# A new issue order for the first 25 slots of a fused top-k attention and feed-forward kernel

## The chip, the cores and the metric

The kernel runs on one core of one Trainium2 chip. Its five engines work side by side, each with an instruction queue of its own: TensorE (PE) multiplies matrices, VectorE (DVE), ScalarE (ACT) and GpSimd (POOL) work on tiles element by element, and SyncE (SP) issues the transfers. The metric is the device time of one execution in microseconds. PSUM is the memory that TensorE writes its products to, SBUF the memory that the other operands lie in.

## The reference

Two blocks follow each other. The first is attention that keeps, for each query, only the 32 largest of its 576 scores. The second is a feed-forward layer with a quick GELU. All is float32.

```python
B, H, S, D = q.shape                      # 8, 8, 576, 64
scores = scale * np.matmul(q, k.transpose(0, 1, 3, 2))
kth = np.partition(scores, -32, axis=-1)[..., -32:-31]
scores = np.where(scores >= kth, scores, -1000000000.0)
scores = scores - np.max(scores, axis=-1, keepdims=True)
attn = np.exp(scores)
attn = attn / (np.sum(attn, axis=-1, keepdims=True) + 1e-09)
attn_out = np.matmul(attn, v)
x = attn_out.transpose(0, 2, 1, 3).reshape(B * S, H * D)   # 4608 x 512
h = x @ w_in                              # 512 x 2048
g = h * (1.0 / (1.0 + np.exp(-1.702 * h)))
out = g @ w_out                           # 2048 x 512
```

## The kernel before

**Slots.** The attention is cut into 144 slots, each of 128 query rows for two heads. For slot n the work passes through all engines, in these steps (the names are those of the code and of this text):

- scores(n) (L468): matmuls on TensorE into two PSUM banks, named c = 0 and c = 1; a bank holds one half of the keys. In the code the four calls for bank 0, each recorded as one step, come before the four for bank 1; the profile counts two matmuls for each call, 16 in all.
- copy_scores(n) (L482): two copies on ScalarE, one for each bank, to the SBUF tile `sc`.
- pair_up(n) (L489): two instructions on VectorE, which take the maximum and the minimum of each pair of keys, one from bank 0 in PSUM and one from the copy of bank 1. The result is the tile `ranked`. Bank 0 can be written again once pair_up(n) and the copy of bank 0 have both read it.
- topk(n) (L509): 14 instructions on VectorE, four rounds of MAX8 (the eight largest) with a MATCH_REPLACE8 (take them out) behind all rounds but the last, for each of the two heads. The first two rounds work on 288 elements, the later ones on 576.
- bounds(n) (L534) on GpSimd works out the cut and the row maximum, mask(n) (L549) and exps(n) (L557) on ScalarE mask and exponentiate, two instructions each, with the sums.
- invert(n) (L568): one small instruction on GpSimd and a reciprocal on VectorE. Up to slot 7 divide(n) (L575) makes two scaled diagonals of it on GpSimd; from slot 8 on normalize(n) (L582) multiplies the probabilities by it on GpSimd.
- Up to slot 7 turn(n) (L590) transposes the probabilities by matmuls on TensorE. From slot 8 on split(n) (L618) copies them apart into 16-bit halves (ScalarE), a transfer writes them to DRAM (`rows<-sc`), and turn_by_dma(n) (L626) brings them back transposed (`pt<-rows`).
- values(n) (L652) or values_at(n) (L685) multiplies them with v on TensorE, and a copy on ScalarE brings the result to `xT`.

Four slots make a block of 128 rows of x. For each block follow hidden (L789; TensorE, h = x @ w_in, into `ph`, or `unit` from slot 25 on), tanh (L814; ScalarE), gate and combine (L826, L843; GpSimd), project (L896; TensorE) and the store of the block. project makes seven products of quarter matrices in place of eight; the matrices that this takes from w_out are made once, by `part` (L877) on GpSimd, the "matrix sums" of the text below, as `raws<-wout,raws`.

**Stages.** opening (L1109) loads and turns the first q and k. slot (L1174) writes the steps of slots 0 to 10, filling_slot (L1339), called by filling (L1375), those of slots 11 to 20 with find (L1303) for the top-k and values_held (L1318) for two slots' values at a time, steady_pair (L1412) those of 21 to 24. From slot 25 on joined_pair (L1599) issues the work directly, in the order in which it is written. stay_warm (L299) issues matmuls whose result nobody reads.

**The order of the first 25 slots.** What opening, slot, filling and steady_pair call on an engine isn't issued at once. Engine and Engines (L123, L138) record each call as a step, 2593 in all. issue_in_order (L1678) then issues them in the order of the table ORDER (L36): a list of step numbers, in which "a+k" is the run of k steps from a. The numbers are those of the order in which the code calls them. Each engine executes its own steps in the order in which the table has them, and a step waits for whatever it depends on that another engine makes. In the trace all recorded steps carry line L133, those issued directly L132.

The lines that decide the order:

```python
        for part in ORDER.split():
            first, _, count = part.partition("+")
            order += range(int(first), int(first) + int(count or 1))
    assert sorted(order) == list(range(len(steps)))
    for i in order:
        steps[i]()
```

BY_DMA is 8 and SETTLED is 10: slot 8 is the first whose probabilities are turned by a transfer, slot 10 the last that slot (L1174) writes.

Of the kernel before, what the change touches and what calls it, by code (L numbers as in the profile page):

```python
# [145 lines left out]
def kernel(  # L146
# [1228 lines left out]
    def filling():  # L1375
# [20 lines left out]

        gate()
        bring_all()
        filling_slot(11, [copy_qk], [], [lambda: values(BY_DMA + 1, put_off), unit], [])
        finish_all()  # L1400
        summing.extend(all_weight_sums())
        filling_slot(12, [bring_all, th], [sums(1)], [put, put, ends_in_turn], [])
# [335 lines left out]
```

## Time and profile before

| | |
|---|---|
| median of 3 runs | 1343.35 us (1343.03 to 1345.45) |
| the profiled execution's own time | 1344.24 us |
| its span in the trace | 1342.4 us |
| mean granted TensorE clock | 0.997 |
| busy: TensorE, VectorE, ScalarE, GpSimd | 1324.3, 1267.8, 1157.6, 979.1 us |
| transfers over the span | 249.27 MB |

The time of an execution holds 1.84 us beside the span of the profile. A row of the timeline has the start in us from the beginning of the span, the time from the start of the row's first instruction to the end of its last one (a row may join some instructions of one kind, "x2"), the engine, the line, the operation, the tiles out<-in with their sizes, and in square brackets how long the engine had stood idle before and what ended that. A row of the windows has the stretch from:to in us, its length, the busy us and the count of instructions of TensorE's matmuls, TensorE's weight loads, VectorE, ScalarE and GpSimd, the granted clock, the busy share of the transfer engines and their GB/s. A row of the grouped instructions has the count, the busy time and the mean ns of one, and the idle time before. A row of the waits names the waiting engine and tile, the engine and tile that ended the wait, and then the time in us, the number of waits and the mean of one. SPq is the queue in which SyncE issues transfers.

### The profile page before, as it was taken

How to read it: one execution, taken by the hardware profiler on the slowest of the kernel's cores; microseconds unless marked ns; L12 is line 12 of the kernel's file. 1: busy time of each engine (PE TensorE's matmuls, PEld its weight loads, DVE VectorE, ACT ScalarE, POOL GpSimd, SP SyncE). 2: the span in 40 equal slices, each digit the busy share in tenths (PEclk: the TensorE clock that was granted, in tenths of full speed). 3: DMA queues.
4: the chain of work that ended last, by engine and by line, in shares of the span. 5: the costliest groups of instructions: out<-in, count | busy, mean ns of one | idle time of the engine just before them, and what ended most of it. 6: DMA issues, size and time to landing. Idle time of an engine off the chain costs nothing.

```text
span 1342.4 us, 54134 instructions
## 1 busy us (share of the span) xinstructions
PE 1324.3 (99%) x22528; PEld 1202.4 (90%) x22528; DVE 1267.8 (94%) x3371; ACT 1157.6 (86%) x1871; POOL 979.1 (73%) x1788
## 2 busy tenths in 40 slices
PE   7999999999999999999999999999999999999998
PEld 5777579899999999999999999999999999999998
DVE  7999999999999999999999999999999999999902
ACT  6999998999999988999999989899989988888831
POOL 3889887777777777777777777777777777777761
PEclk8999999999999999999999999999999999999999
DMA  8444868798989797988999788998899878755640
GB/s 249 157 143 150 197 169 206 195 208 201 219 215 202 170 206 183 230 198 200 204 230 204 186 169 196 230 190 212 176 234 214 189 170 172 186 146 141 148 115 18
DMA packets 532358, 249.27 MB, mean 186 GB/s; under 512 B 463760, under 2 KB 510352, under 8 KB 532112
## 3 DMA queue, kind: packets, MB, share of 16 engines
q1 hardware_dynamic: 531520, 245.38, 78.9%
q8 instruction: 176, 2.88, 0.9%
q14 instruction: 70, 0.57, 0.1%
q10 hardware_dynamic: 592, 0.43, 0.1%
HBM read 46.01 MB, written 104.60 MB: 112 GB/s over the span
## 4 chain that ended last, share of the span: by engine, by line
PE 90%; DVE 4%; ACT 3%; DMA 1%; POOL 1%; issue 1%; DVEq 0%; POOLq 0%; ACTq 0%
PE unit L132 32%; PE po L132 29%; PE mixed L132 12%; PE s_ps L132 7%; PE po L133 4%; DVE ranked L133 2%; PE ph L133 2%; DVE top L133 2%; PE s_ps L133 2%; PE o L133 1%; ACT sc L133 1%; PE tp L133 1%; DMA xT<-rows 1%; ACT raws L133 1%; ACT pr L133 1%
## 5 line engine op out<-in xcount | busy, mean ns | idle before, releaser
L132 DVE MAX8 top<-ranked 128x8 f32<-128x288 f32 (+1 forms) x952 | 517.7, 595 | 0.0
L132 PE MATMUL unit<-xT,win 128*64 128x128 f32 x7936 | 454.2, 273 | 0.0
L132 PEld LDWEIGHTS unit<-xT,win 128*64 128x64 f32 x7936 | 437.4, 137 | 0.0
L132 DVE MATCH_REPLACE8 ranked<-top,ranked 128x288 f32<-128x288 f32 x714 | 383.4, 542 | 0.0
L132 PE MATMUL po<-wout,th 128*64 128x128 f32 x4032 | 329.8, 274 | 0.0
L132 POOL TENSOR_TENSOR th<-th,th 128x128 f32<-128x128 f32 x374 | 273.9, 732 | 29.9
L132 PE MATMUL po<-raws,th 128*64 128x128 f32 x3064 | 252.7, 273 | 0.0
L132 PEld LDWEIGHTS po<-wout,th 128*64 128x64 f32 x4032 | 238.1, 137 | 9.9 <-issue 5.5
L132 POOL TENSOR_SCALAR pr<-pr,rden 128x576 f32<-128x576 f32 x240 | 176.5, 746 | 75.1 <-DVE rden L132 74.4
L132 ACT COPY sc<-pr 128x2304 uint16<-128x2304 uint16 x96 | 205.5, 2141 | 0.9 <-POOL pr L132 0.8
L132 PEld LDWEIGHTS po<-raws,th 128*64 128x64 f32 x3064 | 184.4, 137 | 0.0
L132 ACT ACTIVATE th<-unit 128x512 f32<-128x512 f32 x124 | 74.9, 604 | 94.3 <-PE unit L132 94.3
L132 ACT ACTIVATE pr<-sc,low 128x576 f32<-128x576 f32 x192 | 148.2, 787 | 0.0
L132 ACT ACTIVATE sc<-sc,cut 128x576 f32<-128x576 f32 x192 | 140.8, 797 | 0.0
L132 POOL TENSOR_SCALAR some<-den 128x2 f32<-128x2 f32 x120 | 26.4, 220 | 155.8 <-ACT pr L132 155.4
L132 PE MATMUL s_ps<-qk_t 64*64 64x512 f32 x936 | 139.1, 596 | 0.0
L132 DVE TENSOR_TENSOR ranked<-s_ps,sc 128x576 f32<-128x576 f32 x188 | 132.6, 747 | 0.0
L132 ACT COPY sc<-s_ps 128x1024 f32<-128x1024 f32 x93 | 95.6, 1028 | 33.7 <-PE s_ps L132 32.7
L132 POOL TENSOR_TENSOR th<-th 128x128 f32<-128x128 f32 x250 | 114.7, 459 | 0.4
L133 DVE MAX8 top<-ranked 128x8 f32<-128x576 f32 (+1 forms) x200 | 111.6, 593 | 0.1
L132 POOL TENSOR_TENSOR raws<-raws 128x128 f32<-128x128 f32 (+1 forms) x160 | 89.7, 569 | 8.1 <-ACT raws L132 3.0
L132 POOL TENSOR_SCALAR th<-th 128x512 f32<-128x512 f32 x124 | 76.6, 618 | 13.2 <-ACT th L132 13.1
(145 smaller groups left out, 2178.9 us busy)
## 6 DMA issues: line engine op xcount, KB each, us to landing
rows<-sc SPq DMA_DIRECT2D x112, 576.0 KB, 3.8
rows<-spare SPq DMA_DIRECT2D x24, 576.0 KB, 3.7
qk_rows<-pr SPq DMA_DIRECT2D x23, 576.0 KB, 5.4
out_dram<-raws SPq DMA_DIRECT2D x66, 128.0 KB, 3.3
raws<-in_moe_w_in_dram SPq DMA_DIRECT2D x16, 512.0 KB, 4.9
raws<-in_moe_w_out_dram SPq DMA_DIRECT2D x16, 512.0 KB, 3.9
qk_l<-in_q_dram SPq DMA_DIRECT2D x28, 256.0 KB, 4.9
qk_l<-in_k_dram SPq DMA_DIRECT2D x28, 256.0 KB, 4.6
```

What stands on the lines that cost most here:

```text
L132: return do(*args, **kwargs)
L133: self.engines.collected.append(lambda: do(*args, **kwargs))
```

## The change

The table ORDER gets other contents from about its 120th step on; its first steps and the recorded steps themselves stay, and so does all that is issued directly from slot 25 on. It is a permutation of the same 2593 steps. Counted for each engine, 1171 of TensorE's 1376 steps stand at another place of its queue, 401 of VectorE's 462, 279 of ScalarE's 353, 232 of GpSimd's 273, and none of SyncE's 129. In one line of filling `BY_DMA + 1` becomes `SETTLED - 1`; both are 9. The table has 81 changed lines, of which six from its beginning and two from its end are shown for each side.

```diff
@@ -36,87 +36,87 @@
 ORDER = """
 8 11 0+8 9 12 10 13+5 22 18 23+2 33 25 19 26+5 20 31 34 32 21 38+4 97 35+3 98 42+8 99 50 54+2 100 56+4 53 51
...
-89 133+4 106 96 123 111 124 138+4 107 112 108 125 137 142 126 143 109 144 110 145 127 146+9 128 155 129 163
-208+4 130 156 162 157 167 131 166 158 191 132 175 168 192 171 212 177 159 218 176 172+3 170 182 160 178 213+4
-161 194 169 179+3 183 219 221+2 184 164 185 193 190 195 217 237 224 264 238 226 186 197 189 223 198+3 239 220
-196 266 225 290 227+3 205 230+4 202 307 234+3 204 267 244 269 259+3 265 245 201 308 187 274 291 165 206 293 188
-240 207 251+4 273 289 262 361 275 246+4 255 360 287 241 294 268 250 276 311 280 242 322 366 323+2 256 243 203
-312+3 303 315+4 288 281 309 270+3 340 371 370 358 325 283 326 282 292 327 362 257 263 328 333 329 284 373 258
...
-2562 2561 2563 2572+8 2486 2591+2 2487 2516+2 2590 2564+8 2587 2488 2588 2518+2 2528+2 2489 2589 2530+2 2520+2
-2532+2 2583+2
+89 133+4 106 96 123 111 138+4 107 124 112 108 125 137 126 142 109 143 110 144 127 145+6 128 151+4 162 155 129
+156 130 213+4 163 157 166 131 208+4 194 217 191 132 168 192 158 167 172+3 171 159 175 170 212 176 264 161 218
+177 179+3 195 220 169 221+2 182 230+4 219 223 178 198+3 266 265 160 193 184 237 234+3 245 238 183 185 226 165
+239 190 315+4 186 197 164 227+3 273 224 188 196 290 187 307 189 205 244 246+4 202 225 204 251+4 267 201 259+3
+275 341 269 206 293 291 263 289 411+4 280 241 270+3 361 262 287 274 277+3 282 255 207 362 240 360 370 250 294
+358 268 296 322+2 243 324+4 276 311+4 242 397 297+3 301 309 203 283 304 359 328 288 319+3 284 450 366 281 256
...
+2504 2528+2 2591 2508+2 2485 2510+2 2592 2582 2542 2556+4 2486 2562+2 2552+4 2487 2572+8 2587 2488 2564+8 2588
+2590 2530+2 2589 2489 2512+8 2532+2 2520+2 2583+2
@@ -1396,7 +1396,7 @@
 
         gate()
         bring_all()
-        filling_slot(11, [copy_qk], [], [lambda: values(BY_DMA + 1, put_off), unit], [])
+        filling_slot(11, [copy_qk], [], [lambda: values(SETTLED - 1, put_off), unit], [])
         finish_all()
         summing.extend(all_weight_sums())
         filling_slot(12, [bring_all, th], [sums(1)], [put, put, ends_in_turn], [])
```

146 rows, old and new, of the table ORDER are left out of this document.

## The prediction

> **What bounds the kernel now.** I read the page's shares first, then the windows by stage, then the waits of single engines, and last the timeline around each wait that is left.
>
> ```profile
> span 1342.4 us, 54134 instructions
> PE 1324.3 (99%) x22528; PEld 1202.4 (90%) x22528; DVE 1267.8 (94%) x3371; ACT 1157.6 (86%) x1871; POOL 979.1 (73%) x1788
> PE 90%; DVE 4%; ACT 3%; DMA 1%; POOL 1%; issue 1%; DVEq 0%; POOLq 0%; ACTq 0%
> ```
>
> Two engines are almost full over the whole run, and the chain that ends last is TensorE's. A share over the whole run says little about the first 25 slots, so the next view cuts the span where the work changes.
>
> ```profile
> 112.00:157.00 45.00, 43.87 (x340) 28.39 (x342) 44.97 (x121) 43.83 (x76) 40.07 (x53) 1.00 0.63 173
> 157.00:197.00 40.00, 37.46 (x542) 30.31 (x538) 40.00 (x108) 37.23 (x65) 34.46 (x55) 1.00 0.81 187
> 197.00:247.00 50.00, 49.86 (x948) 45.25 (x952) 48.69 (x131) 44.28 (x70) 38.15 (x71) 1.00 0.77 186
> 247.00:1250.00 1003.00, 1002.80 (x18262) 935.48 (x18256) 1000.65 (x2656) 897.22 (x1409) 736.88 (x1414) 1.00 0.87 196
> ...
> DVE rden L132 <- POOL some L132: 1.7, 6, 0.3
> ```
>
> The columns are PE, PEld, VectorE, ScalarE, GpSimd. From 112 to 197 VectorE is the one that is full (44.97 of 45, 40.00 of 40). From 197 on TensorE is full as well, and from 247 (slot 25, untouched by the change) both are: 1002.80 and 1000.65 of 1003. VectorE waits there six times, 1.7 us in all. So what the new table wins or loses shows at the end one for one, as the time at which TensorE and VectorE together enter slot 25. A win on one of the two alone is worth nothing.
>
> What is there to win? These are VectorE's waits behind the opening:
>
> ```profile
> 32.08 0.76 DVE L133 TENSOR_TENSOR ranked<-s_ps,sc 128x576 f32<-128x576 f32 x1 [0.54 <-ACT sc L133]
> 82.34 0.76 DVE L133 TENSOR_TENSOR ranked<-s_ps,sc 128x576 f32<-128x576 f32 x1 [0.96 <-ACT sc L133]
> 102.01 0.76 DVE L133 TENSOR_TENSOR ranked<-s_ps,sc 128x576 f32<-128x576 f32 x1 [0.31 <-ACT sc L133]
> 221.03 0.76 DVE L133 TENSOR_TENSOR ranked<-s_ps,sc 128x576 f32<-128x576 f32 x1 [1.15 <-ACT sc L133]
> ...
> DVE rden L133 <- POOL some L133: 0.5, 2, 0.4
> ```
>
> That is 0.54 + 0.96 + 0.31 + 1.15 + 0.5 = **3.5 us**, the most that VectorE can gain: its instructions are the same 462 in both tables, so their sum can't change. 0.2% of the time, about what a measurement can tell from no change, is 2.7 us. Four of the waits are pair_up(n), for n = 3, 8, 10 and 23, waiting for the copied scores. TensorE's own wait, just before it becomes full, is this:
>
> ```profile
> 188.77 1.13 PE s_ps L133 x16
> ...
> 190.52 6.48 DMA pt<-rows
> ...
> 197.83 0.22 PE ph L133 x4
> ...
> 197.14 0.57 PE L133 MATMUL o<-pt,v_l 128*64 128x64 f32 x12 [1.41 <-DMA pt<-rows]
> ```
>
> values_at(16) stands still for **1.41 us** until the transposed probabilities of slot 16 have landed. From there to the end TensorE hardly pauses, so its arrival at slot 25 is this landing plus a fixed amount of work.
>
> **The change part by part.** (a) *The literal* `BY_DMA + 1` becomes `SETTLED - 1`: 8 + 1 and 10 - 1 are both 9, so no instruction changes. Cost nothing. (b) *SP's queue*: the 129 recorded DMA issues stand in the same order in both programs, so no transfer moves past another. (c) *Scores.* In the old table the four matmuls of bank 0 always come before those of bank 1. In the new one bank 1 begins first in 19 of the 24 slots from 2 to 25, and its copy to SBUF often stands early: copy_scores(5) of bank 1 is ScalarE's 55th recorded instruction instead of its 72nd, that of slot 3 its 36th instead of its 41st. Bank 0, which pair_up reads directly, is then all that is still to be made when pair_up of the slot before has freed it. What that took where VectorE waited is in the ends of the pair_ups before the four waits:
>
> ```profile
> 25.57 0.75 DVE L133 TENSOR_TENSOR ranked<-s_ps,sc 128x576 f32<-128x576 f32 x1
> ...
> 75.33 1.41 DVE L133 TENSOR_TENSOR ranked<-s_ps,sc 128x576 f32<-128x576 f32 x2
> ...
> 95.70 0.75 DVE L133 TENSOR_TENSOR ranked<-s_ps,sc 128x576 f32<-128x576 f32 x1
> ...
> 212.93 0.74 DVE L133 TENSOR_TENSOR ranked<-s_ps,sc 128x576 f32<-128x576 f32 x1
> ```
>
> From the end of pair_up(n-1) to the start of pair_up(n): 32.08 - 26.32 = 5.76, 82.34 - 76.74 = 5.60, 102.01 - 96.45 = 5.56, 221.03 - 213.67 = 7.36 us. Against that stands the *room*, VectorE's own work between the two. In the new program it is counted with the durations of
>
> ```profile
> L133 DVE MAX8 top<-ranked 128x8 f32<-128x576 f32 x93 | 67.3, 741 | 0.0
> L133 DVE MATCH_REPLACE8 ranked<-top,ranked 128x288 f32<-128x288 f32 x92 | 40.1, 438 | 0.0
> L133 DVE MAX8 top<-ranked 128x8 f32<-128x288 f32 x91 | 38.8, 443 | 0.1
> L133 DVE MATCH_REPLACE8 ranked<-top,ranked 128x576 f32<-128x576 f32 x46 | 33.9, 738 | 0.0
> ```
>
> each less 0.08 us by which neighbours overlap, a replace with 0.06 us for its load: 0.66, 0.42, 0.36 and 0.72 us. At slot 3 a wide maximum and three narrow replaces are added (0.66 + 3 x 0.42): room up 1.9, the wait of 0.54 goes. At slot 23 three wide maxima, one wide replace and three narrow replaces raise it by 4.0 (3 x 0.66 + 0.72 + 3 x 0.42): the 1.15 goes. At slots 8 and 10 the room falls a little (4.9 to 4.6, 5.4 to 4.6). There it is the early bank 1 that must save 1.0 us; 16 score matmuls take 1.13, so doing half of them and a copy ahead saves about 1.1 to 1.2, an estimate from that row. The 0.96 and 0.31 should go, with little to spare. (d) *Slot 5* gets worse. There bank 0's copy now stands behind the first mask of slot 3:
>
> ```profile
> 50.10 0.24 POOL L133 TENSOR_SCALAR cut<-top 128x4 f32<-128x4 f32 x1
> ...
> 51.07 1.45 ACT L133 ACTIVATE sc<-sc,cut 128x576 f32<-128x576 f32 x2
> ...
> 51.45 0.74 DVE L133 TENSOR_TENSOR ranked<-s_ps,sc 128x576 f32<-128x576 f32 x1
> ```
>
> Half of the masks (0.72) and a copy from 51.07 on end at 52.4, while pair_up(5), with 0.74 us more ahead of it and 0.54 less waiting, would start at 51.65. Bounds: nothing, if ScalarE runs earlier, or 0.7 lost. I take 0.6, since the mask can't start before the cut at 50.34. So VectorE stands 0.54 + 0.96 + 0.31 + 0.4 (the first reciprocal) - 0.6 = 1.6 us earlier at slot 16. (e) *TensorE's wait at 197.* The new order puts all of scores(21) (16 matmuls, 1.13 us) before values_at(16) and two steps of hidden (4 matmuls, 0.22) behind it: 0.91 us of the 1.41 is filled with work. The other 0.5 goes if the landing comes 0.5 us earlier. Its chain:
>
> ```profile
> 175.85 2.52 POOL L133 TENSOR_TENSOR raws<-wout,raws 128x512 f32<-128x512 f32 x2
> ...
> 180.25 0.87 POOL L133 TENSOR_TENSOR th<-th 128x128 f32<-128x128 f32 x2
> ...
> 182.20 1.47 POOL L133 TENSOR_SCALAR pr<-pr,rden 128x576 f32<-128x576 f32 x2 [0.78 <-DVE rden L133]
> ...
> 183.70 2.12 ACT L133 COPY sc<-pr 128x2304 uint16<-128x2304 uint16 x1
> ...
> 185.85 0.35 SPq L133 DMA_DIRECT2D rows<-sc  x1
> ...
> 190.52 2.89 SPq L133 DMA_TRANSPOSE pt<-rows  x1
> ```
>
> GpSimd's normalize(16) gets two more matrix sums ahead and three combining steps fewer (2 x 1.26 - 3 x 0.43 = 1.2 us later), but it had waited 0.78 for the reciprocal. That reciprocal gets two more narrow maxima ahead (0.7), and ScalarE's split(16) one copy fewer. With 1.6 gained on VectorE the reciprocal is 0.9 earlier, GpSimd is late by 1.2 - 0.78 = 0.4 if nothing ahead of it moves, and earlier by up to 0.9 if it follows VectorE. Bounds for the landing: 0.4 later to 1.2 earlier. I take 0.5 earlier, about the middle. So the whole wait of 1.41 goes, and TensorE is then held by its own work. More could come only from its smaller pauses between 150 and 175. (f) *197 to 247* must let VectorE follow. Its 1.15 at slot 23 is there for that.
>
> **Sum:** -0.9 (work into the wait) - 0.5 (earlier landing) = **-1.4 us**. The profiled execution took 1344.24 (span 1342.4), so 1342.8 in its terms; the median of the runs is 0.89 lower, so I predict 1343.35 - 1.4 = **1342.0**.
>
> [...] TensorE's order in slots 1 to 4, warm-up matmuls included, is shuffled most.
>
> ```profile
> 24.00:28.00 4.00, 1.54 (x4) 0.70 (x5) 4.00 (x10) 3.14 (x9) 3.68 (x5) 0.72 0.99 339
> 28.00:32.00 4.00, 4.00 (x23) 2.44 (x23) 3.54 (x9) 3.26 (x7) 3.54 (x7) 0.50 1.05 390
> 32.00:36.00 4.00, 3.90 (x29) 3.27 (x27) 3.92 (x13) 4.00 (x8) 3.26 (x4) 0.93 0.47 184
> 44.81 1.40 DVE L133 TENSOR_TENSOR ranked<-s_ps,sc 128x576 f32<-128x576 f32 x2
> ```
>
> The granted clock falls to 0.72, then 0.50, then is back at 0.93: TensorE is idle there and works at half rate until about 32. The new order has scores(3), half of scores(4) and then nothing until turn(0), so the slow stretch may last to 36. turn(0), 16 matmuls in about 1.8 us there, would take 1.8 longer. Scores(4) has room for that before pair_up(4) at 44.81, but the copies of turn(0) stand in ScalarE's queue ahead of exps(1), and so of the second reciprocal. [...]
>
> **The rivals.** *A, everything fits:* all 3.5 us of VectorE's waits go and TensorE's small pauses shrink too. For: bank 1 ahead is what the four waits lacked. Against: TensorE must gain as much, and only 1.41 of its wait is one piece. Time 1343.35 - 3.2 = 1340.1. *B, no gain:* the slow clock costs VectorE 1.8 less the 0.5 of wait that goes at slot 3, 1.3, or the landing comes no earlier while slot 5 waits. Time 1343.4. *C, slower: rooms too small.* In the new order the room falls from 10.1 to 4.9 at slot 9, 7.5 to 3.4 at 11, 6.3 to 3.6 at 19 and 8.3 to 4.8 at 22. If bank 0 still needed the 5.6 us of slots 8 and 10, because TensorE or ScalarE reaches it late in its own queue, slots 11 and 19 alone would lose 2.2 + 2.0. It decides from the point where bank 0's scores don't start within 2 us of pair_up's end. Time 1343.35 - 1.4 + 4.2 = 1346.2. For: both engines are 93% busy or more between 157 and 197. Against: at 11 and 19 pair_up no longer waits for bank 0's copy, which stands behind it.
>
> **How the numbers follow.** Forecast 0.45 (1340.8 to 1343.0), A 0.18, B 0.19, C 0.18. The range takes in A with all 3.5 us (1339.85) and C's single time: 1339.9 to 1346.2. Faster by over 0.2% (under 1340.66) is A: 0.18. Slower by over 0.2% (over 1346.04) is most of C: 0.15, since C may also cost a little less than its 4.2. The rest, 0.67, is within 0.2%.
>
> **What would show it.** Right: no wait of values_at(16) for the transposed rows, and TensorE full about 1.4 us earlier; no waits at pair_up 3, 8, 10 and 23; a wait of half a microsecond at 5; the first `unit` matmul of slot 25 about 1.4 earlier; the same windows from there. Wrong: new waits of VectorE on the copied scores at 9, 11, 19 or 22 (C), or a granted clock below 0.9 between 32 and 36 with a later second reciprocal (B).

## The result, and the profile after

The changed kernel takes **1346.89 us** (median of 10 executions, 1345.04 to 1351.7) against 1343.40 (10 executions, 1342.73 to 1345.45). The ratio is 1.0029, 95% interval 1.0018 to 1.0039: it is slower, by 0.29% or some 3.9 us (the two medians lie 3.5 apart). Its executions also lie further apart, over 6.7 us in place of 2.7. The profiled execution took 1347.04 us, its span is 1345.2.

First the windows of the changed kernel, with the columns of before:

```profile
112.00:157.00 45.00, 42.57 (x305) 27.56 (x306) 44.62 (x123) 42.65 (x71) 40.61 (x51) 1.00 0.61 173
157.00:197.00 40.00, 39.04 (x556) 31.46 (x556) 38.79 (x104) 37.26 (x67) 34.76 (x54) 1.00 0.82 185
197.00:247.00 50.00, 49.37 (x922) 44.19 (x920) 48.51 (x129) 45.69 (x73) 38.20 (x75) 1.00 0.76 196
247.00:1250.00 1003.00, 1002.52 (x18268) 935.79 (x18266) 1000.49 (x2658) 897.12 (x1410) 734.77 (x1411) 1.00 0.86 196
```

From 247 to 1250 TensorE and VectorE are busy for as long as before, to 0.3 us; TensorE has one new wait there, 0.48 for a landing at 1015. VectorE, full before from 112 to 197, now has gaps (44.62 of 45, 38.79 of 40). So most of this execution's loss must be in the time at which the two engines enter slot 25. These rows are the first pair_up of the execution, pair_up(26) (the first that is issued directly) and the first `unit` matmul; before, then after:

```profile
9.86 1.42 DVE L133 TENSOR_TENSOR ranked<-s_ps,sc 128x576 f32<-128x576 f32 x2 [2.78 <-ACT sc L133]
...
246.24 1.41 DVE L132 TENSOR_TENSOR ranked<-s_ps,sc 128x576 f32<-128x576 f32 x2
...
252.05 3.66 PE L132 MATMUL unit<-xT,win 128*64 128x128 f32 x64
```

```profile
10.62 1.42 DVE L133 TENSOR_TENSOR ranked<-s_ps,sc 128x576 f32<-128x576 f32 x2 [2.78 <-ACT sc L133]
...
248.54 1.42 DVE L132 TENSOR_TENSOR ranked<-s_ps,sc 128x576 f32<-128x576 f32 x2
...
254.69 1.48 PE L132 MATMUL unit<-xT,win 128*64 128x128 f32 x24
```

The first row differs by 0.76 between two executions of the same code, so it is taken off: VectorE enters (248.54 - 10.62) - (246.24 - 9.86) = **1.54** later than before, TensorE (254.69 - 10.62) - (252.05 - 9.86) = **1.88** later. The span is 2.8 longer, and 0.76 of that is the chance of the opening. Now VectorE's waits, from its timeline:

```profile
53.78 0.76 DVE L133 TENSOR_TENSOR ranked<-s_ps,sc 128x576 f32<-128x576 f32 x1 [1.45 <-ACT sc L133]
85.45 1.42 DVE L133 TENSOR_TENSOR ranked<-s_ps,sc 128x576 f32<-128x576 f32 x2 [0.43 <-ACT sc L133]
103.16 0.76 DVE L133 TENSOR_TENSOR ranked<-s_ps,sc 128x576 f32<-128x576 f32 x1 [0.25 <-ACT pt L133]
124.00 0.76 DVE L133 TENSOR_TENSOR ranked<-s_ps,sc 128x576 f32<-128x576 f32 x1 [0.38 <-ACT sc L133]
158.64 0.17 DVE L133 RECIPROCAL rden<-some 128x2 f32<-128x2 f32 x1 [0.81 <-POOL some L133]
194.42 0.76 DVE L133 TENSOR_TENSOR ranked<-s_ps,sc 128x576 f32<-128x576 f32 x1 [0.40 <-ACT sc L133]
212.51 0.76 DVE L133 TENSOR_TENSOR ranked<-s_ps,sc 128x576 f32<-128x576 f32 x1 [0.34 <-ACT sc L133]
235.90 0.76 DVE L133 TENSOR_TENSOR ranked<-s_ps,sc 128x576 f32<-128x576 f32 x1 [1.08 <-ACT sc L133]
```

They are the pair_ups of slots 5, 8, 10, 12, the reciprocal of 13, and the pair_ups of 20, 22 and 24: 5.1 us, where before had 3.5. The waits at 3 and 23 are gone. TensorE's waits behind 150 us:

```profile
156.84 0.32 PE L133 MATMUL o<-pt,v_e 128*64 128x128 f32 x1 [1.69 <-ACT qk_t L133]
178.93 0.32 PE L133 MATMUL o<-pt,v_e 128*64 128x128 f32 x1 [0.88 <-ACT qk_t L133]
229.01 0.46 PE L133 MATMUL o<-pt,v_e 64*64 64x64 f32 x10 [0.48 <-DMA pt<-rows]
```

The wait of 1.41 for the landing of slot 16 is gone, and there is one for the landing of slot **19** at 229. It is the smallest of the three, and the one whose removal gave the time back (e10_landing below). The same landing in before: split(19) on ScalarE, the issue of the transposing transfer, and the matmuls of values_of_two(18, 19) that read it.

```profile
210.27 2.14 ACT L133 COPY sc<-pr 128x2304 uint16<-128x2304 uint16 x1
...
216.36 6.00 SPq L133 DMA_TRANSPOSE pt<-rows  x1
...
227.16 0.40 PE L133 MATMUL o<-pt,v_e 64*64 64x64 f32 x14
```

and after, with what ScalarE does ahead of split(19):

```profile
212.63 0.79 ACT L133 ACTIVATE sc<-sc,cut 128x576 f32<-128x576 f32 x1
213.50 0.78 ACT L133 ACTIVATE pr<-sc,low 128x576 f32<-128x576 f32 x1
...
214.28 0.76 ACT L133 ACTIVATE pr<-sc,low 128x576 f32<-128x576 f32 x1
...
215.04 2.10 ACT L133 COPY sc<-pr 128x2304 uint16<-128x2304 uint16 x1
...
220.60 4.83 SPq L133 DMA_TRANSPOSE pt<-rows  x1
```

From the end of split(19) to the first matmul that needs its result there were 227.16 - 212.41 = **14.7 us** before. Now there are 229.01 - 0.48 - 217.14 = **11.4**, because the second mask and the exponentials of slot 20 stand ahead of split(19), while TensorE wants the result only 1.4 later (228.53 in place of 227.16) and split(19) ends 4.7 later. The transfer took 11.9 in this execution. In before it landed 7.9 after its issue at 216.36, which is 11.9 behind split's end as well; there 2.9 were to spare, and here nothing.

### The profile page after: what moved, and what is told of

It is laid out like the page before. It is cut to its first block, busy times and chain, and to the rows that moved or that the text cites. A ratio compares the mean times of both kernels' runs of the same rounds, so it can differ in the third digit from the quotient of the medians.

```text
span 1345.2 us, 54141 instructions
## 1 busy us (share of the span) xinstructions
PE 1328.0 (99%) x22528; PEld 1204.1 (90%) x22528; DVE 1267.9 (94%) x3371; ACT 1159.0 (86%) x1871; POOL 978.3 (73%) x1788
## 4 chain that ended last, share of the span: by engine, by line
PE 82%; DMA 1%; ACT 0%; SPq 0%; issue 0%; DVE 0%; DVEq 0%
PE unit L132 32%; PE po L132 29%; PE mixed L132 12%; PE s_ps L132 7%; DMA pt<-rows 1%; PE ph L133 1%; PE po L133 0%; PE o L133 0%; SPq L132 0%; DMA rows<-sc 0%; ACT sc L133 0%; PE s_ps L133 0%; ACT pr L133 0%; DVE raws L132 0%; DVEq L1733 0%
```

## The experiments

Two theories stood against each other. **V**: VectorE's waits for the copied scores and the reciprocal add up, and their sum is the loss. **T**, later narrowed to **L**: TensorE decides, by a landing. The steps of both tables are the same 2593, and after equal counts the two have issued almost the same set, so one table can be cut and continued by the other. In the table below "later" is worked out for each kernel as above, from the same three rows of its profile. "Span" is how much longer the whole profiled execution was than that of before, with the opening taken off in the same way; what it holds beyond the two columns ahead of it was lost, or won, behind slot 25.

| kernel | VectorE later | TensorE later | span | ratio to before (95%) | executions, us |
|---|---|---|---|---|---|
| after | 1.54 | 1.88 | 2.0 | 1.0029 (1.0018 to 1.0039) | 1345.04 to 1351.70 |
| e12_again (after once more) | 2.60 | 2.93 | 3.8 | 1.0030 (1.0018 to 1.0042) | 1345.16 to 1351.79 |
| e1_first | 1.41 | 1.43 | 2.2 | 1.0010 (1.0001 to 1.0018) | 1344.41 to 1347.80 |
| e2_middle | 3.66 | 3.66 | 4.2 | 1.0024 (1.0013 to 1.0034) | 1346.62 to 1349.62 |
| e3_last | 5.71 | 6.05 | 5.7 | 1.0035 (1.0022 to 1.0047) | 1346.99 to 1351.34 |
| e4_moved | 0.52 | 1.12 | 4.4 | 1.0021 (1.0012 to 1.0030) | 1344.10 to 1349.24 |
| e5_more | 3.45 | 4.05 | 5.5 | 1.0013 (1.0004 to 1.0022) | 1343.12 to 1349.55 |
| e9_split | -0.45 | -0.11 | 0.5 | 1.0008 (1.0000 to 1.0017) | 1344.10 to 1347.96 |
| e10_landing | 0.93 | 1.27 | 0.6 | 1.0007 (0.9999 to 1.0016) | 1344.55 to 1347.62 |
| e11_late | 4.97 | 4.97 | 5.3 | 1.0034 (1.0022 to 1.0046) | 1347.93 to 1350.01 |
| e6_copies | -1.12 | -1.12 | -1.6 | 1.0008 (0.9999 to 1.0017) | 1342.49 to 1347.55 |
| e7_scores | -1.12 | -1.12 | -1.5 | 1.0000 (0.9991 to 1.0008) | 1341.53 to 1344.42 |
| e8_both | -1.44 | -1.44 | -2.0 | 0.9993 (0.9985 to 1.0002) | 1341.70 to 1343.79 |
| e13_both_again | -0.23 | -0.22 | 0.6 | 0.9992 (0.9983 to 1.0001) | 1342.34 to 1345.43 |

### A third of the table at a time: e1_first, e2_middle, e3_last

```diff
-the old table, 2593 steps
+e1_first:  new table for steps 0..651, the rest in the old order
+e2_middle: old for 652 steps, new up to step 1290, the rest in the old order
+e3_last:   old for 1291 steps, the rest in the new order
```

> The new table for the first 652 of the 2593 steps (to about 75 us, the top of slot 6), then the remaining steps in the old order. Theory V (VectorE's own waits decide): of the five microseconds of waits in the new program this part holds the 1.45 at the pair_up of slot 5 and not the old 0.54 at slot 3, so VectorE is 0.9 later at slot 7; if nothing later absorbs it, the time is 0.9 above before (about 1344.3), and if the old wait of 0.96 at slot 8 absorbs it, 0 to 0.3 above. Theory T (TensorE's order decides, by transfers that land late and by more changes between kinds of matmuls, all behind 100 us): no difference, 1343.4.

> The old table for 652 steps, the new one up to its 1291st (about 75 to 148 us, slots 7 to 13), then the rest in the old order. Theory V: the waits here are 0.43, 0.25 and 0.38 in place of 0.96, 0.38 and 0.31, so 0.6 below before (1342.8). Theory T: TensorE changes its kind of matmul 79 times in this part in place of 62; at 0.1 us for a change up to 1.7 more for TensorE, and the transposed probabilities of slot 11 land later: 0.5 to 1.7 above before (1343.9 to 1345.1).

> The old table for 1291 steps (to about 148 us), then the new one to its end. Theory V: new waits of 0.40 at the pair_up of slot 20, 0.34 at 22 and 1.08 between the halves of 24, and not the 1.15 at 23 and 0.16 at a reciprocal: 0.5 above before (1343.9), and 1.3 above if the reciprocal of slot 13 waits 0.8 as well. Theory T: the wait of 1.41 for the probabilities of slot 16 goes, and TensorE changes its kind 164 times in place of 157: 0.7 below before (1342.7) by its two terms.

The 0.1 us that theory T reckons for a change of kind stands in these rows of before's trace at a change of form:

```profile
42.25 0.83 PE L133 MATMUL po<-ident 128*128 128x128 f32 x6
42.92 1.06 PE L133 MATMUL tp<-xT,pr 128*128 128x128 f32 x8
43.81 0.83 PE L133 MATMUL po<-ident 128*128 128x128 f32 x6
44.58 0.56 PE L133 MATMUL o<-pt,v_l 128*64 128x128 f32 x3
```

Six 128*128 matmuls take 0.67 us up to the start of the next row where that has the same form, and 0.77 where it has the form 128*64; the first of the two is a change of kind as well, from `po` to `tp`, and shows no 0.1.

The last part alone costs 0.35%, no less than the whole change, so most of the cause is to be looked for behind 148 us. The first costs 0.10%. The parts can't be added up (0.69% against 0.29%), since a cut table can lose time of its own. e2_middle's 0.24% says little of the new table: pair_up(8) waited 2.96 there, at the seam of the two tables, where the old one waits 0.96 and the new one 0.43. e3_last entered slot 25 some 3 to 4 us later than the whole change did: TensorE waited 2.44 at 156.76, where it waits 1.69 in the new table. It also waited 2.22 for the landing of slot 19, with the granted clock at 0.63 from 230 to 234, and VectorE waited 2.14 and 1.96 at the two halves of pair_up(24) behind it:

```profile
231.30 0.70 PE L134 MATMUL o<-pt,v_e 64*64 64x64 f32 x10 [2.22 <-DMA pt<-rows]
```

(All lines are one number higher in kernels whose table is one line longer.)

### VectorE's waits taken away: e4_moved

```diff
-copy of bank 0 (slot 5), pair_up(5)
+pair_up(5) first half, mask(3) second half, copy of bank 0
-copy of bank 0 (slot 20), pair_up(20)
+pair_up(20), copy of bank 0
-copy of bank 0 (slot 24), pair_up(24) second half
+pair_up(24) second half, copy of bank 0
```

> The new table with three moves: at slots 5 and 20 the copy of bank 0 is issued behind pair_up (at 5 one mask later, at 20 behind both halves), and at slot 24 the second half of pair_up is issued ahead of that copy. Nothing else moves. Theory V: the waits of 1.45, 0.40 and 1.08 go, so VectorE enters slot 25 up to 2.9 earlier; with 0.3 to 0.5 of new waits behind them 2.4 below the changed kernel (about 1344.5 where it takes 1346.9). Theory T: TensorE's order is the same, so no change from the changed kernel (1346.9), and VectorE's waits come back elsewhere.

(At slot 20 the copy now stands behind split(17) on ScalarE.) The waits at 5, 20 and 24 went. Others came to 3.7 us in all, as in before, and VectorE entered slot 25 only 0.52 later than before. TensorE entered 1.12 later, and the time hardly moved: 1.0021, of the new table's 1.0029. V alone doesn't hold. In this profile TensorE waited 1.06 for slot 19's landing. But neither wait explains this execution: 3.3 of its 4.4 us were lost behind slot 25, in work that the table doesn't order. There TensorE waited 1.97 for another transposed landing, and then ran at a reduced granted clock:

```profile
1014.99 1.56 PE L133 MATMUL mixed<-pt,v_l 128*64 128x128 f32 x16 [1.97 <-DMA pt<-rows]
...
1012.00:1016.00 4.00, 2.03 (x34) 1.79 (x32) 2.88 (x8) 2.60 (x7) 0.99 (x3) 0.93 1.13 313
1016.00:1020.00 4.00, 4.00 (x48) 2.10 (x44) 4.00 (x14) 0.79 (x1) 3.75 (x7) 0.64 1.02 242
```

By these rows the clock cost an estimated 1.7 beside the wait (0.07 + 0.36 of 4 us each). At the same place before's TensorE didn't wait, and the other profiles have between nothing and 1.62 (e5_more). So the end doesn't follow slot 25 one for one, and whether a later entry makes such waits likelier no run shows.

### The landing: e5_more, e9_split, e10_landing, e11_late, e12_again

```diff
 e5_more: e4_moved, and
-ScalarE: copy of bank 0 (slot 15), copy_qk_ends
+ScalarE: copy_qk_ends, copy of bank 0 (slot 15)
-GpSimd:  gate, bounds(20), combine, normalize(19)
+GpSimd:  normalize(19), gate, bounds(20), combine
 e9_split: e5_more, and
-ScalarE: mask(20) second half, exps(20), split(19)
+ScalarE: split(19), mask(20) second half, exps(20)
 e10_landing: the new table with only the moves of normalize(19) and split(19)
 e11_late: the old table with
-ScalarE: split(19), mask(20), ..., exps(20) first half
+ScalarE: mask(20), ..., exps(20) first half, split(19)
```

> The three moves of e4_moved and two more. ScalarE's copy of bank 0 of slot 15 goes one place back, behind a copy_qk_ends for which TensorE waited 1.41 at 153 us in e4_moved (values_at(11)); GpSimd's normalize(19) goes ahead of a gate, for the landing for which TensorE waited 1.06 at 226 us. Theory V (VectorE's waits decide): only the reciprocal's wait of 0.81 at slot 13, which hangs on the same copy, goes: VectorE enters slot 25 0.8 earlier than in e4_moved, and the end follows it. Theory T (TensorE decides where it enters slot 25 later than VectorE, as in the profile of e4_moved: 1.41 against 0.52 later than before): TensorE gains 1 to 2, and both enter at about the time of before, 1.1 earlier than in e4_moved. By both the time is near before (1343.5 to 1344.5).

> e5_more and one move on ScalarE: split(19) goes ahead of the second mask and the exponentials of slot 20. In the new table TensorE's values_of_two(18, 19) begins 10 us behind the end of split(19), in the old one 14 us; the transposed probabilities took 12 to 14 us from there to land in the profiles so far, and TensorE waited 0.48 to 2.62 for them. Theory L (what the new table loses, and what makes its executions spread, is this landing): the landing comes about 2.6 earlier, the wait is below 0.5, no wait of 2.6 at the pair_up of slot 24 behind it, and the time is 1 to 1.5 below e5_more's (1343.0 to 1343.8), its executions as close together as those of before (within 4 us). Theory V (VectorE's other waits decide): 0.4 lower at most, the same spread as e5_more (6 us).

> The new table with only the moves for that landing: normalize(19) ahead of a gate on GpSimd, split(19) ahead of the second mask and the exponentials of slot 20 on ScalarE. All waits for the copied scores stay. Theory L: 1.5 to 2.5 below the new table (e12_again), and a narrower spread. Theory V: VectorE's waits of 1.45, 0.81, 0.40 and 1.08 are untouched, so within 0.5 of the new table.

> The old table with one thing of the new one: split(19) goes behind the first exponential of slot 20 on ScalarE (some 4 us later), so that about 10 us are left until values_of_two(18, 19) in place of 14; the issues of SyncE that stood between go with it. Theory L: TensorE waits 0.5 to 2.6 at this place, 0.5 to 2 above before, with a wider spread. Theory V: no difference from before, since no wait of VectorE for scores is touched.

> The new table as it is, once more, beside the others on the same chip, as what e9_split and e10_landing are compared with, and for a second profile. All theories: 3 to 4 above before. Theory L: executions from 1 to 8 us above the fastest of before, and in the profile a wait at values_of_two(18, 19) other than the 0.48 of the first one, with the end following it; theory V: the same VectorE waits as in the first profile, to 0.2.

e5_more held its first half: the reciprocal of slot 13 no longer waits, since copy_qk_ends, and behind it TensorE and exps(13), no longer stand behind a copy that waits for pair_up(15). But normalize(19) ahead of the gate brought split(19) forward by little, because ScalarE still had slot 20 ahead of it. In its profile, the slowest of its executions, the landing took 13.9 and TensorE waited 2.62. Behind the wait the granted clock was 0.52 (230 to 234), and both engines entered slot 25 2.9 later than in e4_moved, though the wait was only 1.56 longer:

```profile
226.00:230.00 4.00, 2.16 (x38) 2.07 (x40) 2.70 (x7) 0.00 (x0) 4.00 (x8) 0.63 0.41 155
230.00:234.00 4.00, 4.00 (x64) 4.00 (x62) 2.67 (x5) 2.60 (x6) 0.72 (x2) 0.52 0.54 112
```

(This run's recorded expectation puts TensorE of e4_moved at 1.41 later than before; by the rows it is the 1.12 of the table.)

e12_again, the new table once more, shows how this place varies. TensorE, ScalarE's copy behind x_of_two and VectorE wait in turn:

```profile
214.11 2.10 ACT L134 COPY sc<-pr 128x2304 uint16<-128x2304 uint16 x1
...
219.74 6.38 SPq L134 DMA_TRANSPOSE pt<-rows  x1
...
229.77 0.46 PE L134 MATMUL o<-pt,v_e 64*64 64x64 f32 x10 [2.17 <-DMA pt<-rows]
...
231.35 0.27 ACT L134 COPY xT<-o 128x128 f32<-128x128 f32 x1 [2.92 <-PE o L134]
...
232.19 0.76 DVE L134 TENSOR_TENSOR ranked<-s_ps,sc 128x576 f32<-128x576 f32 x1 [1.02 <-ACT sc L134]
236.65 0.76 DVE L134 TENSOR_TENSOR ranked<-s_ps,sc 128x576 f32<-128x576 f32 x1 [1.65 <-ACT sc L134]
```

The order is the same to the instruction; only the transfer took 13.6 us in place of 11.9, against the 11.4 that there are. Both engines entered slot 25 1.1 later than in the first profile (2.60 against 1.54, 2.93 against 1.88).

e10_landing is the strongest evidence. Its views at the same place:

```profile
211.08 2.12 ACT L134 COPY sc<-pr 128x2304 uint16<-128x2304 uint16 x1
...
217.00 5.87 SPq L134 DMA_TRANSPOSE pt<-rows  x1
...
227.36 0.46 PE L134 MATMUL o<-pt,v_e 64*64 64x64 f32 x10 [0.38 <-ACT th L134]
```

The time from split's end to the first use is 227.36 - 0.38 - 213.20 = 13.8, and no wait for the transfer is left. On the same chip the median falls from 1348.70 (e12_again) to 1345.56, and the executions lie within 3.1 us in place of 6.6. Moves of three instructions give back 3.1 of the 3.7 us, with 4.4 us of VectorE's waits still there. The two at pair_up(24), 1.02 and 1.65 in e12_again, went along, so they hung on the same place. In the two profiles the spans differ by 3.3, of which 1.7 at slot 25. The other 1.6 lie behind it, where e12_again waited 0.90 for a landing at 704 and 0.27 at 1017, and e10_landing not; whether that belongs to the change is open. e9_split, which has e5_more's other moves too, is no better (1.0008), though both engines enter slot 25 1.4 earlier in its profile than in e10_landing's.

e11_late is the converse: the old table with 10.7 us at this place loses 0.34%. It is more than the landing alone. TensorE waited 0.95 for the transfer and 1.42 for ScalarE, the granted clock was 0.68 from 230 to 234, and the late split held up ScalarE and so the reciprocals, by 1.70 at slot 20 and 2.40 at slot 22. So it shows that the position of split(19) on ScalarE costs that much, not how much of it is the transfer.

### The prediction's terms by themselves: e6_copies, e7_scores, e8_both, e13_both_again

```diff
 e6_copies: the old table; slots 8, 10 and 23
-ScalarE: copy of bank 0, ... (pair_up behind it)
+ScalarE: copy of bank 0 behind the second half of pair_up
 e7_scores: the old table
-TensorE: values_at(16), 2 steps of hidden, scores(21)
+TensorE: 2 steps of hidden, scores(21), values_at(16)
 e8_both and e13_both_again: both
```

> The old table with three moves on ScalarE alone: at slots 8, 10 and 23 the copy of bank 0 goes behind the second half of pair_up. pair_up there waited 0.96, 0.31 and 1.15 for the last of the two copies. Theory V: these waits fall by 1.9 (0.6 of slot 23 stays, for the copy of bank 1), VectorE enters slot 25 up to 1.9 earlier and the time falls by as much if TensorE follows. Theory T: TensorE still waits until 197 us for the probabilities of slot 16 and is full from there, so VectorE's gain is given back: no difference, or up to 0.5 from an earlier landing.

> The old table with one move on TensorE alone: the 16 matmuls of scores(21) and two steps of hidden go ahead of values_at(16), into the wait of 1.41 before it. This is the term of 0.9 in the prediction by itself. Theory T: TensorE enters slot 25 0.9 to 1.4 earlier; the time falls by that if VectorE follows. Theory V: VectorE's waits are what they were (scores(21) isn't what it waits for), so its arrival and the time don't change.

> e6_copies and e7_scores together. If each engine alone is given back to the other, as theory T has it, this is the only one of the three that gains: both engines enter slot 25 0.9 to 1.4 earlier, 1.2 below before. By theory V it is the same as e6_copies.

> e8_both once more. Its first interval against before reached from 0.15% below to 0.02% above. If the 1.4 that both engines were earlier at slot 25 in its profile is in every execution, it is again 0.7 to 1.4 below before (0.05 to 0.1%); if that profile was only a good execution, no difference from before.

In the profiles both engines entered slot 25 1.12 earlier with either edit alone. That was expected of neither theory: the two waits hang together. With e7_scores the scores of slot 23 came earlier, and VectorE's wait of 1.15 there went; with e6_copies the landing of slot 16 came earlier, and TensorE's wait at 197 went. In the times neither gain shows (1.0008 and 1.0000): e7_scores' interval has room for the 1.12, that of e6_copies hasn't. e8_both, measured twice on two chips, is 0.07% and 0.08% below before, each interval ending 0.01 to 0.02% above no difference. It is faster than the changed kernel, and at most some two microseconds faster than before. Its second profile entered only 0.23 earlier, with 0.84 of wait at the reciprocal of slot 22 and 0.33 of TensorE for the landing of slot 19, so the first profile's 1.44 isn't there in every execution.

## Why the prediction was wrong

- **The step that failed** is under "What is there to win": behind the landing of slot 16 "TensorE hardly pauses, so its arrival at slot 25 is this landing plus a fixed amount of work", and (f), which asked of the stretch from 197 to 247 only whether VectorE can follow. The new table shortened the time for the landing of slot 19 from 14.7 to 11.4 us, and a transfer that took 11.6 to 13.9 (e11_late, e5_more) then ended last. No wait stood there before, so no row of before pointed at it; the new order of ScalarE did. Moving split(19) and normalize(19) forward again (e10_landing) returned 3.1 of the 3.7 us that the new table loses beside it. The forecast gain of 1.4 didn't come even so (1.0007); where it went is shown in part only, by the bullets below.
- **(e)** was right on its wait and wrong on what follows. The 1.41 went (0.49 was left in e12_again). TensorE still arrived later: its wait behind copy_qk_ends rose from 0.68 (at 154.24) to 1.69, and its listed waits from 150 to 247 sum to 3.05 in place of 3.36. The term by itself (e7_scores) was worth 1.12 at slot 25 in a profile and nothing that can be seen in the time.
- **(c)** held at slots 3 and 23. At 8 and 10 waits of 0.43 and 0.25 stayed. Not seen: the waits at 12, 20, 22 and at the second half of pair_up(24), 0.34 to 1.08 each. The last one has its copy of bank 0 between the two halves and behind a split on ScalarE.
- **(d)** named the right place, and its 0.6 was 1.45 in the first profile, 0.53 in the second:

```profile
52.50 0.76 DVE L134 TENSOR_TENSOR ranked<-s_ps,sc 128x576 f32<-128x576 f32 x1 [0.53 <-ACT sc L134]
```

- **The sum for VectorE**, 1.6 earlier at slot 16, came out as 3.3 of waits up to there (1.45 + 0.43 + 0.25 + 0.38 + 0.81) in place of 2.2. By e4_moved and e10_landing this decides little: with 1.4 less of VectorE's waits the ratio went from 1.0029 to 1.0021, within the intervals; without the wait for the landing, and with VectorE's in place but for those at pair_up(24), to 1.0007.
- **"A win on one of the two alone is worth nothing"** was too simple: e6_copies and e7_scores each moved one engine's queue and brought both engines to slot 25 earlier. That what is won there **shows at the end one for one** didn't hold either (e4_moved, and e9_split beside e10_landing).
- **Rival C** had the sign and not the place. The rooms it called too small were enough: no wait at 9, 11 and 19, and 0.34 at 22. That the time, 1346.89, came out near C's 1346.2 is chance.
- **Rival B and the clock.** The granted clock fell earlier and was back earlier than feared. The first three rows are of the changed kernel's first profile, the others of e12_again, the same order:

```profile
24.00:28.00 4.00, 3.41 (x18) 2.54 (x19) 3.94 (x12) 4.00 (x12) 3.67 (x5) 0.50 1.02 352
28.00:32.00 4.00, 4.00 (x31) 2.46 (x30) 4.00 (x12) 2.52 (x5) 3.49 (x5) 0.66 1.03 385
32.00:36.00 4.00, 3.66 (x34) 2.90 (x32) 4.00 (x13) 4.00 (x7) 3.59 (x6) 1.00 0.60 204
...
24.00:28.00 4.00, 3.71 (x36) 2.41 (x36) 3.92 (x12) 4.00 (x12) 3.68 (x5) 1.00 1.03 333
28.00:32.00 4.00, 2.34 (x23) 2.32 (x21) 4.00 (x12) 3.46 (x6) 3.51 (x5) 1.00 1.04 387
32.00:36.00 4.00, 3.15 (x34) 2.40 (x34) 4.00 (x11) 4.00 (x8) 3.84 (x7) 1.00 0.59 195
```

0.50, 0.66 and 1.00 in the three stretches where before had 0.72, 0.50 and 0.93: the slow stretch is not longer. In e12_again the clock didn't fall at all, nor in e1_first, whose first part is the same. Where it fell, pair_up(5) waited 1.45; in those two, and in e10_landing with 0.63, 0.94 and 1.00, it waited 0.51 to 0.53. So the slow stretch seems to account for some 0.9 of the 1.45, and for most of what (d) had too small; one profile is all that shows it. All eight profiles with the old opening have a slow stretch and five of the seven with the new one have none, so rival B had it the wrong way round; the mean granted clocks of these executions are 0.995 to 0.997 with the old opening and 0.997 to 1.000 with the new one. The clock fell behind pauses of TensorE of 1.97 (e4_moved, at 1015), 2.69 (the changed kernel, at 24.59) and 2.96 us (before, at 26.46), and didn't behind one of 2.17 (e12_again, at 229.77).

Open: the 0.07% that e10_landing keeps (its interval includes none); what decides over the waits behind slot 25; and how many executions of the new table lose at the landing, since only the profiled ones can be looked into. Of the others only the mean granted clock is known: the 8 of the new table's 19 executions with 0.997 took 1349.5 us on average, the 11 with more 1347.1, which fits the waits with a slow clock behind them and doesn't say at which place.

## What to carry to other kernels

When an order is changed, write down for each transfer the time from its last producer to its first use, before and after, and hold it against the longest time that the profiles show for it; a wait of zero today says nothing of the room behind it. A share or a sum of waits doesn't show such a place, and one profile shows a single draw of it (here 11.9 and 13.6 us in two executions of one order); compare the profile's span with the place where the change ends, too, since an execution can lose its time behind it. Where the executions of a kernel lie further apart than those of the one before (here 6.6 us in e12_again, 3.1 in e10_landing), look for a landing without room.

## What the runs showed of the hardware

- The same transposing transfer, from split's end to TensorE's first matmul, took 11.6 (e11_late) to 15.5 us (e13_both_again) where TensorE waited for it, and its issue on SyncE's queue 4.83 to 6.65. In e13_both_again, whose order here is that of before, its write was issued 1.7 behind split's end, after another transposing transfer, and TensorE waited 0.33: the old order's room isn't always enough either. With 2.4 more of room than in the new table the executions lay within 3.1 us in place of 6.6 (e10_landing).
- A pause of TensorE can cost more than itself: behind waits of 1.97 (e4_moved, at 1015), 2.22 (e3_last) and 2.62 us (e5_more) the granted clock was 0.52 to 0.64 in at least one of the next stretches of 4 us. Behind the 2.17 of e12_again it stayed at 1.00.
- pair_up reads bank 0 and the copy of bank 1, not the copy of bank 0; yet where ScalarE's copy of bank 0 comes first in the table and pair_up waited, it started 0.03 us behind that copy's end (53.75 and 53.78 at slot 5, 235.87 and 235.90 at slot 24 of the changed kernel), and the other way round the copy waited:

```profile
156.04 0.64 ACT L133 COPY sc<-s_ps 128x576 f32<-128x576 f32 x1 [0.83 <-DVE ranked L133]
```

  This copy waited 0.83 for the second half of pair_up(15), and started 0.04 behind its end at 156.00; copy_qk_ends, TensorE (1.69) and the reciprocal of slot 13 (0.81) waited behind it. In the first 25 slots of before no copy of scores overlaps a pair_up; in those of the changed kernel three do, by up to 0.72, all of them copies of bank 1 (slots 4, 7 and 11). The copy of bank 0 and pair_up both read bank 0 and share the tile `sc`, and no run tells which of the two makes them wait.
- The first pair_up of the execution starts 9.38 us (e8_both) to 10.62 us (the changed kernel) into the span, by the same instructions. Differences below a microsecond between single spans are not to be read before this is taken off.
